# A written-out engine program reordered: about a hundred tasks of block-sparse attention and a squared-ReLU MLP at other places, twelve on other engines

## Chip, cores and metric

The kernel runs on one core of one Trainium2 chip. The metric is the device time of one launch in microseconds (us), lower is better. The core has five engines with a queue each: TensorE (PE, matmuls; PEld is its weight load), VectorE (DVE), ScalarE (ACT), GpSimd (POOL) and SyncE (SP), which here only issues DMAs. POOL issues DMAs too.

## What is computed

Attention of 4 batches, 8 heads, 768 tokens and head size 64, with a block mask (blocks of 32 tokens; a block sees its neighbours, the first and last block, and three sampled blocks), then an MLP with a squared ReLU, 512 to 2048 to 512:

```python
scores = scale * np.matmul(q, k.transpose(0, 1, 3, 2))
mask = np.abs(blk_i - blk_j) <= window
mask = mask | (blk_i == 0) | (blk_j == 0) | (blk_i == n_blocks - 1) | (blk_j == n_blocks - 1)
for qb in range(n_blocks):
    for kb in sampled_blocks[qb]:
        mask[qb * block:(qb + 1) * block, kb * block:(kb + 1) * block] = True
scores = np.where(mask, scores, -1000000000.0)
# softmax over the keys
x = matmul(attn, v), heads side by side: (3072, 512)
h = x @ w_in; r = np.maximum(h, 0.0); g = r * r
return g @ w_out
```

## The kernel before

**Units and batches.** A unit is a pair of heads of one batch: units 0 to 3 are batch 0, 4 to 7 batch 1, 8 to 11 batch 2, 12 to 15 batch 3. Batches 0 and 1 compute all 768 by 768 scores and mask the exponentials. Batches 2 and 3 are sparse: six visits of 128 queries each, for which the keys (`k_gather`, copies on POOL or DVE) and the values (`v_gather`, `v_window`, DMAs from a copy of v in DRAM written by `v_store`) are gathered.

**Getting q, k and v in.** `load` (L150, L152) brings a unit's q, k or v as float32 to SBUF (pools qs, ks, vs), `cast_qk` (L124, L122) makes it bfloat16 in one of four buffers qc, taken in turn, and from unit 4 on `transp_dma` (L313) transposes it by DMA into the resident tile QKT, which frees the qc buffer. Units 0 to 3 are transposed on TensorE (`transp`, L306) and copied out (`evac`). `cast_v` fills VB.

**Attention.** `scores` or `s_scores` (TensorE into one of four PSUM tiles X of two banks), `exps` or `s_exps` on ACT (L358, L624), `masks` or `s_masks` on DVE (L365, L631), then `values` or `s_values` (L204, L396, L654), and `normalize` or `s_normalize` on DVE; the result goes to xT, in batches 1 to 3 through a transposing DMA (L438, L667).

**MLP.** For each of 12 tiles of 256 tokens: 16 tasks `hidden` (four matmul pairs each, xT times w_in), four `relu` (L708 on ACT or L710 on DVE), `square` (L719 ACT, L721 POOL or DVE), 8 tasks `output` (g times w_out), `out_copy` and `store`. The weights come by `w_load` on POOL: pieces 0 and 1 of w_in (L329), 2 to 5 of w_out (L332). The MLP of one batch runs between the attention tasks of the next.

**The order is written out by hand.** The body builds 1224 tasks with their dependencies and buffers, and a string PROGRAM says in which order they are issued. Each word is a letter for the engine (P TensorE, V VectorE, A ScalarE, G GpSimd, S SyncE), the task's number, and for tasks that take a PSUM tile its index after a slash. Every engine runs its own words in that order. Buffers of a pool other than X are handed out in the order of the words, so the order also decides whose release a task waits for:

```python
if b.pool == "X":
    b.at = int(spot)
else:
    b.at = len(taken[b.pool]) % bufs[b.pool]
```

**Tasks named below.** 605 to 636 prepare batch 3: for units 12, 13, 14 and 15 the loads of q, k and v are 605 to 607, 613 to 615, 621 to 623 and 629 to 631; the casts of k and q are 608 and 610, 616 and 618, 624 and 626, 632 and 634; their transposes 609 and 611, 617 and 619, 625 and 627, 633 and 635; the casts of v 612, 620, 628 and 636. 637 and 638 are batch 3's `v_store`. 587 and 565 are `v_window` of batch 2's visits 5 and 4, and 691 of batch 3's visit 2. 642 is the `k_gather` for batch 3's first visit. 571 and 577 are `s_scores` of units 9 and 11 in visit 4, 595, 598, 601 and 579 `s_masks` of batch 2. 986 is a `relu` and 1022 a `hidden` of batch 2's MLP, 980 an `out_copy`. 711 and 712 are the two `v_gather` of batch 3's visit 3, 690 one of visit 2; 700 and 719 are `s_scores` of batch 3. 38 and 39 cast and transpose the later tokens of unit 0's q; 54 casts unit 2's k; 89 copies out a part of the mask; 77 is `w_load(3)`; 793 and 794 are two half `square` tasks.

Of the kernel before, what the change touches and what calls it, by code (L numbers as in the profile page):

```python
# [25 lines left out]
def kernel(  # L26
# [940 lines left out]
    for T in TILES:  # L967
# [48 lines left out]
        P223/3 P203/2 A238 V245 P805 S275 V272 A224 P229/1 P204 P806 S276 A230 V225 S273 G266 P286/3 A823 P807 V231 P808 A287 V205
        P232/1 A829 V270 P206 P289/3 P233 S271 V239 P809 A290 V208 V234 P296/2 V288 S253 A810 P246/3 V291 P235 S437 P247 A297 V236
        P299/0 V248 P830/1 P831 A300 V280 P302/2 V278 P832 A303 S279 P249 P283/0 P833 V250 V298 P852/3 A284 V434 V834 P314/2 S277
        P853 A315 P846/0 S281 V304 P847 A835 P311/1 V285 P854 P855 V258 A312 P848 V301 S269 P849 A856 S21 G282 P292/2 P864/1 V316
        S454 A850 P293 S436 V313 P305/3 P865 V295 A857 G851 P308/0 P306 A309 P866 V307 P353/2 P867 A354 P326/3 G439 V868 P858/0 P859  # L1020
        A327 P320/2 P860 V274 A321 P323/1 V310 S438 P836/3 S444 G441 A324 P861 S460 P347/2 P837 V496 A862 V355 V322 P317/1 A348
        P350/0 S445 V328 P318 V325 G443 P838 S811 V319 A351 V349 P329/2 A869 P334/1 P330 V352 P839 V331 A335 V23 P356/0 S333 A863
        P340/2 P840 A341 P841 G447 P362/1 P357 G459 P842 A363 S452 G449 P337/2 S442 P843 A338 P870/1 A844 S446 V345 P359/2 S448 P871
        A360 V342 V358 P374/3 S462 P872 V339 A375 S440 V336 P365/0 P377/2 V361 P873 A366 V364 P343/3 A378 S450 V367 P371/0 P344 P874
        A372 V346 S845 V376 P368/2 P398/3 V373 P369 A399 P875 S461 V379 S453 V370 P380/0 V470 P401/3 P381 A402 P385/2 V382 P876 V400
        S384 P391/0 P16/3 P877 V451 A392 V403 P404/3 V878 P886/0 A405 P887 A386 V406 G463 P388/1 P425/3 P24/2 P888 A389 G467 V27 V25
        P889 A426 P880/1 P881 S613 G465 A890 S631 P428/3 P882 S469 G455 P883 A429 P407/0 S464 V427 V26 A884 P408 P422/3 V396 A891
        V409 P926/1 P927 V457 A423 P928 V390 S468 P929 A885 V424 P892/2 S456 P893 A930 V387 P413/0 P894 V393 A414 P895 P898/3 V896
        A931 P899 S614 P394/1 P416/0 V430 S466 P395 A417 P900 V397 P932/2 P901 A897 S458 G471 P933 V902 V539 P410/1 P934 A411 G473
        S615 P935 P904/0 S605 V415 A936 P431/3 V502 A903 P905 S472 P432 P476/1 P481/2 P906 A477 V418 A482 P914/1 V412 V433 S621 P915  # L1030
        V498 V541 G499 G937 P419/2 V478 P916 V483 P486/3 P917 A487 P907 A918 P491/3 P420 A492 P479/1 P908 A480 P489/3 P474/1 V421
        P909 A490 V493 S435 A475 P484/2 V488 P910 V545 A485 P911 A919 G503 P920/3 V912 G542 S501 P494/1 G616 P921 G500 V519 P507/2
        P7/0 P922 A508 V495 P513/0 G626 P923 S879 A514 P948/2 V582 S913 G636 P949 A924 S544 P510/1 V515 P504/0 P950 V509 A511 P951
        G620 A505 P954/3 V952 P955 S623 G546 A925 P938/1 S606 S622 V512 P556/0 P939 G523 A557 S497 V506 P553/2 P940 A554 P956 P547/0
        P957 V524 A548 P941 G543 S617 V958 P516/2 V549 S627 P525/0 V558 V584 P942 A526 V517 P550/3 A959 P943 G588 A953 P944 S518
        P528/0 A551 P966/2 P967 A529 V552 P945 V555 S522 G520 P960/3 A946 P968 G618 P531/0 P961 A532 P969 G608 S629 P962 V970 P534/1
        P963 G624 S630 A535 P559/0 V665 A971 V530 S625 G521 P994/2 V589 V562 P995 A964 G566 P988/1 P989 P996 S619 P990 P590/3 G965
        S607 P997 A591 P991 G586 A998 P972/3 G563 P973 A999 V560 P1000/2 V610 P1001 S561 P974 V533 V536 P1002 S609 V992 G628 P593/0
# [3 lines left out]
        P643/0 V667 P1007 V603 A644 P1008 S604 V570 V576 S641 V671 P655/3 P1031 A656 G640 P1034/0 A1032 P1035 V579 P1009 P1036 P1037  # L1042
        P648/3 P1010 A1038 P580/1 A649 G668 A1033 P645/0 P658/3 V688 V581 P1011 A659 V672 P1012 S583 A646 P650/1 P1016/3 A651 P660/0
        P1017 A661 P653/1 P1013 V647 A654 V662 V657 V652 P1018 V692 A1014 P1019 P663/0 V751 A1020 S1015 G693 A1039 P676/1 V664 V710
        P679/2 P1050/3 A677 S670 P1051 A680 G669 P1056/0 P1052 A1021 V681 P1057 P682/1 P1053 S666 A683 P1062/2 V1054 P1063 P1058
        P673/1 S712 P1064 A674 P1059 P1040/3 A1055 V1060 P1065 P1068/1 V684 A1061 P1069 V675 P694/0 P1041 V678 A1066 V714 G715 P1070
        A695 G689 P685/2 A1067 P1071 S981 V753 V686 P703/0 P1042 A1072 S687 P700/2 A704 P1043 V1073 A701 G690 P722/1 P697/0 S756
        P1044 A723 V702 V735 A698 P1045 P716/2 P1046 A717 S713 P725/1 V696 P1047 P1074/0 S691 A1048 P1090/2 A726 P1091 P1084/3 P1085
        S1049 P719/1 P1092 A720 G757 S711 P1075 P1086 V758 P1096/1 V705 P1093 V718 P1097 A1094 V721 P1087 V699 P1098 P1076 A1095
        G736 P1099 A1088 P1102/2 V1100 P1077 P1103 V727 A1101 P706/3 S754 P743/1 V731 P1078 V707 G732 A744 P1104 V724 A1089 P728/3  # L1050
        P1105 V729 P768/1 P1079 A1106 S730 P740/3 G755 A769 P1080 A741 P762/2 S709 P1081 A763 P765/1 P1108/3 V764 A766 S733 V770
        P759/2 P1109 V1082 A760 P746/1 A1107 P1110 V761 V745 A747 P1132/2 V767 P1118/0 V742 S734 P1119 V748 P1133 P1111 P1120 P737/1
        P1134 A738 P1135 P1121 V739 A1136 P1112 V1122 P1139/1 A1137 G1138 P771/2 G1124 P749/0 V772 P1113 G1123 V750 S773 P1140
# [38 lines left out]
```

## Time and profile before

| | us |
|---|---|
| median of three runs | 255.13 |
| the three runs | 257.79, 255.13, 254.16 |
| the profiled execution | 257.6 |
| its span, first to last instruction | 255.9 |
| TensorE busy / idle in the span | 243.9 / 12.0 |
| ACT, DVE, POOL busy | 187.0, 166.3, 106.1 |
| mean granted TensorE clock | 0.992 |

In rows of the waits, "A <- B: total, times, longest" says that A stood idle until B released it; "issue" is time in which nothing that the profile shows was waited for. A row of a timeline has the start, the time, the engine, the line, the operation, out<-in and a count, and in brackets the idle time before it with its releaser. A row of stretches has the stretch, its length, the busy time of TensorE, weight load, DVE, ACT and POOL with their counts, then the granted clock, the share of the DMA engines and GB/s. SPq and POOLq are the parts of an engine that issue DMAs. The 1.7 us between the execution and its span lie before the first and behind the last instruction.

### The profile page before, as it was taken

To read this page: it belongs to the slowest core of one execution; us is meant where nothing else is said; L and a number is where in the kernel's file an instruction comes from. 1 tells how busy PE (TensorE), PEld (TensorE's weight loads), DVE (VectorE), ACT (ScalarE), POOL (GpSimd) and SP (SyncE) were. 2 spreads that over 40 slices of the span, in tenths; PEclk is the share of its full clock that TensorE was granted. 3 is DMA by queue.
4 is the path that set the end of the run, shared out by engine and by line. 5 is a ranking of instruction groups with operands and counts; after the bars stand their busy time and mean duration, and the time that the engine had idled before them with its cause. 6 is when DMAs were issued, how large, how long until landed. Compare 5 with 4: busy or idle time off the path is not lost.

```text
span 255.9 us, 12281 instructions
## 1 busy us (share of the span) xinstructions
PE 243.9 (95%) x5265; PEld 182.1 (71%) x5265; DVE 166.3 (65%) x394; ACT 187.0 (73%) x220; POOL 106.1 (41%) x231
## 2 busy tenths in 40 slices
PE   7988999899999999998999996999999999999994
PEld 4667889679865667776867774867965775776683
DVE  7667997689799989896654964357464555441300
ACT  3898999899998789965867663669887569415241
POOL 3165533010534032579426983347475445140020
PEclk9999999999999999999999999799999999999999
DMA  6999999999899999999999999952548924243022
GB/s 192 356 279 182 200 235 219 254 225 210 238 304 196 258 180 261 160 263 166 287 236 164 178 204 176 259 150 57 158 101 178 219 63 105 66 123 87 3 85 86
DMA packets 64950, 47.10 MB, mean 184 GB/s; under 512 B 32367, under 2 KB 59376, under 8 KB 64896
## 3 DMA queue, kind: packets, MB, share of 16 engines
q1 hardware_dynamic: 58736, 38.02, 67.2%
q0 software_dynamic: 5472, 7.85, 17.1%
q8 instruction: 41, 0.67, 1.1%
q10 hardware_dynamic: 688, 0.46, 0.6%
q14 instruction: 13, 0.11, 0.1%
HBM read 35.51 MB, written 7.91 MB: 170 GB/s over the span
## 4 chain that ended last, share of the span: by engine, by line
PE 73%; DMA 11%; DVE 5%; issue 3%; ACT 2%; POOL 1%; DVEq 1%; SPq 1%; POOLq 0%; ACTq 0%
PE X L204 68%; PE X L654 4%; DMA w_out_sb<-in_moe_w_out_dram 4%; DMA qs<-in_q_dram 3%; DMA KG<-in_k_dram 2%; DMA QKT<-qc 2%; ACT pT L358 1%; DVE r L710 1%; DVE pT L365 1%; DVE qc L124 1%; PE X L396 1%; DVEq L558 1%; POOL g L721 1%; SPq L170 1%; ACT r L708 1%
## 5 line engine op out<-in xcount | busy, mean ns | idle before, releaser
L204 PE MATMUL X<-xT,w_in_sb 64*128 64x256 bf16 x1536 | 99.9, 272 | 1.5 <-DVE r L710 1.2
L204 PE MATMUL X<-w_out_sb,g 64*128 64x512 bf16 (+3 forms) x960 | 95.4, 334 | 1.9 <-issue 1.0
L204 PEld LDWEIGHTS <-w_in_sb 64*128 64x128 bf16 x1536 | 75.4, 95 | 14.8 <-issue 1.9
L358 ACT ACTIVATE pT<-X 128x1024 bf16<-128x1024 f32 x72 | 70.7, 1036 | 7.1 <-PE X L204 5.6
L204 PEld LDWEIGHTS <-g 64*128 64x128 bf16 x960 | 39.4, 94 | 27.9 <-issue 2.4
L624 ACT ACTIVATE pT<-X 128x768 bf16<-128x768 f32 (+1 forms) x56 | 41.3, 767 | 24.5 <-PE X L204 23.9
L719 ACT ACTIVATE g<-r 128x1024 bf16<-128x1024 f32 (+1 forms) x45 | 41.7, 941 | 7.8 <-DVE r L710 7.7
L708 ACT ACTIVATE r<-X 128x1024 f32<-128x1024 f32 x28 | 29.8, 1076 | 14.8 <-PE X L204 14.7
L365 DVE TENSOR_TENSOR pT<-pT,VG 128x1024 bf16<-128x1024 bf16 x60 | 39.6, 696 | 1.5 <-ACT pT L358 1.4
L710 DVE TENSOR_SCALAR r<-X 128x1024 f32<-128x1024 f32 x20 | 24.5, 1223 | 22.8 <-PE X L204 20.7
L581 POOL DMA_DIRECT2D VG<-rows x54 | 27.2, 507 | 22.2 <-issue 8.8
L631 DVE TENSOR_TENSOR pT<-pT,MKS 128x768 bf16<-128x768 bf16 (+1 forms) x48 | 28.2, 624 | 12.3 <-ACT pT L624 11.1
L204 PE MATMUL X<-QKT 64*128 64x256 bf16 (+1 forms) x384 | 32.3, 254 | 2.0 <-issue 0.9
L721 POOL TENSOR_TENSOR g<-r 128x512 bf16<-128x512 f32 (+1 forms) x14 | 16.9, 1220 | 31.2 <-ACT r L708 14.3
L204 PEld LDWEIGHTS <-QKT 64*128 64x128 bf16 x384 | 17.0, 97 | 6.7 <-issue 2.8
L124 POOL CAST VB<-vs 128x768 bf16<-128x768 f32 x10 | 8.4, 842 | 25.5 <-DMA vs<-in_v_dram 25.4
L204 PEld LDWEIGHTS <-pT 64*128 64x128 bf16 x768 | 15.3, 94 | 3.5 <-DVE pT L365 0.2
L204 PE MATMUL X<-VB,pT 64*128 64x65 bf16 x768 | 17.0, 190 | 0.1
L204 PEld LDWEIGHTS <-KG 64*128 64x128 bf16 x528 | 13.5, 95 | 5.0
L204 PE MATMUL X<-QKT,KG 64*128 64x64 bf16 x528 | 15.1, 190 | 0.0
L578 POOL DMA_INDIRECT VG<-rows,idx x9 | 9.0, 1004 | 13.5 <-DMA QKT<-qc 7.7
L124 POOL CAST qc<-ks 128x384 bf16<-128x384 f32 (+1 forms) x15 | 8.0, 566 | 14.6 <-DMA ks<-in_k_dram 12.4
(106 smaller groups left out, 216.1 us busy)
## 6 DMA issues: line engine op xcount, KB each, us to landing
vs<-in_v_dram SPq DMA_DIRECT2D x14, 384.0 KB, 5.0
ks<-in_k_dram SPq DMA_DIRECT2D x13, 384.0 KB, 6.4
qs<-in_q_dram SPq DMA_DIRECT2D x12, 384.0 KB, 4.7
out_dram<-ys SPq DMA_DIRECT2D x9, 512.0 KB, 5.8
VG<-rows SPq DMA_DIRECT2D x20, 132.0 KB, 4.0
w_in_sb<-in_moe_w_in_dram POOLq DMA_DIRECT2D x2, 1024.0 KB, 9.3
w_out_sb<-in_moe_w_out_dram POOLq DMA_DIRECT2D x4, 512.0 KB, 9.4
VG<-rows POOLq DMA_DIRECT2D x54, 33.0 KB, 3.2
```

The lines of the kernel that those rows point to most:

```text
L124: (V if e == "DVE" else G).tensor_copy(out=out, in_=in_)
L204: last = nc.tensor.matmul(out(r ^ crossed), lhsT(r ^ crossed, rows), rhs(r ^ crossed, rows), skip_group_check=True, **kw)
L358: A.activation(out=pT[:, :, 0:n], in_=stile.pop(a)[:, :, 0:n], func=AF.Exp, scale=scale)
L365: V.tensor_tensor(out=pT, in0=pT, in1=m[:, None].broadcast_to([P, 2, len(cs), w]), op=AOP.mult)
L581: (G if e == "POOL" else sy).dma_start(out=to[j * HB:(j + 1) * HB], in_=pairs[bass.ds(r * HB, HB)])
L624: A.activation(out=pT[:, :, 0:n], in_=stile.pop((u, v, gs))[:, :, 0:n], func=AF.Exp, scale=scale)
L631: V.tensor_tensor(out=pT, in0=pT, in1=m[:, None].broadcast_to([P, 2, n]), op=AOP.mult)
L654: nc.tensor.matmul(po[i * D:(i + 1) * D, h, a * VW:(a + 1) * VW], pts[g][:, h, c * D:(c + 1) * D], val, start=a == 0 and c == 0, stop=c == ...
L708: A.activation(out=to, in_=src, func=AF.Relu)
L710: V.tensor_scalar(out=to, in0=src, scalar1=0.0, scalar2=None, op0=AOP.max)
L719: A.activation(out=g, in_=r, func=AF.Square)
L721: (G if e == "POOL" else V).tensor_mul(out=g, in0=r, in1=r)
```

## The change

Only PROGRAM changes: all 1224 tasks remain, with the same dependencies. The indices of the PSUM tiles are permuted throughout. Twelve tasks go to another engine: 54 (`cast_qk`), 912 (`out_copy`) and 992 (`relu`) from DVE to ACT; 89 (`mask_evac`) and 1072 (`relu`) from ACT to DVE; 256, 278 and 457 (`cast_qk`) from DVE to POOL; 455 (`cast_qk`) and 628 (`cast_v`) from POOL to DVE; 443 (`cast_v`) from POOL to ACT; 712 (`v_gather`) from SyncE to POOL. About a hundred keep their engine and stand elsewhere in its queue, most of them a few places away.

On SyncE, from the load of unit 15's q on, the order

    629 630 625 619 607 561 609 611 540 633 587 635 565 637 638 947 604

becomes

    629 607 609 619 630 561 611 625 540 587 633 565 637 638 947 635 604

and further on 712 leaves, and 691 moves from behind 713 to ahead of 687. On VectorE `632 634 708 595 986 598 601 980 573` becomes `628 632 595 986 708 598 601 980 579 634 573`. On TensorE `977 599 978 979 571 1022 1028 1029 1023 577` (with 574 ahead of 977) becomes `977 599 574 978 571 577 979 1028 1029 1022`. On POOL `787 793 794 77` becomes `787 794 77 793`, `690 757` becomes `690 712 757`, and 38 goes from behind 73 to ahead of 49.

The lines of the diff that hold these places:

```diff
-    P4/3 P9/1 P125/3 V41 A116 P2/1 P106/2 V3 G52 A126 G74 G63 P5/0 V107 P123/1 P65/0 A124 P108 P121/3 V66 V110 G49 P82/0 A122
-    P84/2 P131/1 V83 G60 V85 P135/0 A132 G73 P86/3 P117/2 V87 A136 G38 P88/1 G75 P10/3 P133/3 V118 A89 P61/0 A134 G78 P119 V62
-    P12/1 P90/1 V120 P168/0 G76 P15/2 P39/3 A91 P174/2 V40 A169 P127/1 G70 A175 P137/3 V128 P144/0 V138 P129 P147/2 A145 V130
+    A114 G64 P9/2 P125/0 P2/2 A116 V3 G52 P106/3 A126 P5/2 P123/1 V107 G63 P65/2 A124 P108 P121/0 V110 G74 V66 P82/3 A122 P84/1
+    V83 G38 P131/2 V85 P135/3 A132 P86/0 P117/1 V87 A136 G49 P10/2 V118 P88/0 P133/2 G60 V89 P12/3 A134 G73 P61/3 P119 P90/0 V62
+    A91 P39/2 G75 V120 P168/3 V40 P174/1 A169 P127/0 G78 P137/2 G76 A175 V128 P144/3 G70 V138 P129 P147/1 A145 V130 V176 P15/0
...
-    V160 A216 P98/2 P190/0 V163 A99 P212/3 V792 A780 P164/2 A213 S81 V191 P795/1 G793 A779 V165 P796 P209/3 G794 P192 P166 S259
-    S260 P797 A210 V167 V193 P798 P824/2 V217 V214 V383 A799 G77 P825 P197/0 P194/3 P826 G801 A198 P827 P818/1 A195 V828 G254
+    S251 S252 P190/3 V163 A99 P212/2 V792 A780 P164/1 A213 V191 P795/0 G794 A779 V165 P796 P209/2 P192 P166 P797 G77 A210 V167
+    V193 V214 P798 V217 S81 P824/1 G793 V383 A799 P825 P194/3 P826 A195 G801 P827 S259 S260 P197/2 S267 P818/0 A800 V828 G254
...
-    P963 G624 S630 A535 P559/0 V665 A971 V530 S625 G521 P994/2 V589 V562 P995 A964 G566 P988/1 P989 P996 S619 P990 P590/3 G965
+    P966/2 P967 A529 V552 P945 V555 G520 P960/1 A946 S522 P968 G618 P531/3 P961 A532 P969 G624 P962 S629 V970 P559/0 G608 S607
...
-    P1003 G585 A594 S611 V527 A1004 G612 G564 A993 P537/1 V567 A1005 P982/0 V639 P983 P596/2 P975 V538 A597 P984 V592 S540 P976
-    V632 P568/2 P985 S633 A569 V634 P574/1 P977 V708 V595 P599/2 P978 V986 A600 S587 P979 A575 V598 S635 A987 V601 P571/2 V980
-    A572 S565 P1022/0 V573 P1028/1 P1029 S637 P1023 S638 P577/3 P1030 A578 G642 P1024 S947 P1025 P1006/2 A1026 P602/3 A1027
+    P1003 P537/2 S625 A1004 P982/0 V639 V538 A993 P983 P596/3 V592 P975 A1005 S540 G585 V628 V632 P984 A597 P976 G612 S587 V595
+    P568/2 P985 A569 P977 S633 V986 V708 P599/3 P574/2 P978 A600 V598 S565 G564 A575 V601 P571/0 P577/3 P979 A572 A578 V980
+    P1028/2 A987 P1029 S637 V579 V634 S638 S947 V573 P1022/0 S635 P1030 P1023 P1031 G642 P1024 A1032 P1025 P1006/3 A1026 P602/1
...
-    P673/1 S712 P1064 A674 P1059 P1040/3 A1055 V1060 P1065 P1068/1 V684 A1061 P1069 V675 P694/0 P1041 V678 A1066 V714 G715 P1070
+    P1045 V1073 P719/1 G712 P716/0 S756 P1046 V724 A717 V702 P725/3 A720 P1047 V735 S713 P1074/0 A1048 P1090/1 A726 V696 P1091
...
-    P1044 A723 V702 V735 A698 P1045 P716/2 P1046 A717 S713 P725/1 V696 P1047 P1074/0 S691 A1048 P1090/2 A726 P1091 P1084/3 P1085
+    P1059 A674 P1064 V1060 P1040/2 A1055 P1065 V684 A1061 S981 P1068/0 V714 G715 G689 S691 P1069 A1066 P694/1 V675 P1041 V678
```

More of the change, by code (lines that the diff above doesn't have):

```diff
@@ L1016 @@
[L1016 to L1023, printed above, removed]
@@ new lines @@
+        P139 P71/0 A148 V140 P171/3 V170 P781/2 P782 V72 A172 V146 P92/1 P187/0 P783 V93 A188 P784 V173 P50/3 P181/1 A785 P177/0
+        V189 V51 A182 P141/2 G786 V178 P774/3 P775 A142 V149 P184/1 P179 P776 G79 G22 V180 A185 P94/2 P777 V143 P155/0 A95 V778 G787
+        P150/1 A156 P158/2 V151 P161/3 A159 P788/0 V183 P152 P789 S80 V186 A154 P215/2 A162 P790 V157 P14/1 P791 V160 A216 P98/1
+        S251 S252 P190/3 V163 A99 P212/2 V792 A780 P164/1 A213 V191 P795/0 G794 A779 V165 P796 P209/2 P192 P166 P797 G77 A210 V167
@@ new lines @@
+        V193 V214 P798 V217 S81 P824/1 G793 V383 A799 P825 P194/3 P826 A195 G801 P827 S259 S260 P197/2 S267 P818/0 A800 V828 G254
+        P819 A198 G256 P226/3 S255 P820 A227 P200/1 V196 P812/2 V211 P813 S257 A201 P243/3 V199 P821 P814 A244 V264 P218/1 P815 S265
+        A822 P219 P802/3 A816 V220 S268 V202 P240/0 P221 P803 A241 V228 P96/2 P804 A222 V97 A817 S261 P237/0 V262 P223/1 P203/2 A238
+        V242 S263 P805 V245 A224 P229/0 P204 S275 P806 A230 V225 V272 P286/1 A823 P807 V231 S276 V205 S273 P808 A287 G266 P232/0
@@ new lines @@
+        A829 P289/1 V270 P233 V239 P206 P809 A290 S271 V208 V234 P296/2 A810 P246/1 V288 S253 P235 P247 G278 V236 S437 A297 P299/3
+        P830/0 V291 S279 P831 A300 V248 P302/2 P832 V280 A303 S277 P249 P283/3 V250 P833 V298 S281 P852/1 A284 V434 V834 P314/2 P853
+        A315 P846/3 V304 P847 A835 P311/0 V285 P854 V258 P855 A312 P848 V301 S269 P849 S21 A856 V316 P292/2 V313 P864/0 A850 P293
+        G282 P305/1 V295 A857 P865 S454 G851 P308/3 S436 P306 A309 P866 V307 P353/2 P867 A354 P326/1 G439 V868 P858/3 P859 A327
@@ new lines @@
+        P320/2 P860 V274 A321 P323/0 V310 S438 P836/1 S444 V355 A324 P861 S460 V322 P347/2 S445 P837 V496 A862 G441 P317/0 A348
+        P350/3 V328 P318 V325 S811 P838 A351 V319 V349 P329/2 A869 P334/0 V352 P330 P839 V331 A335 V23 P356/3 S333 A863 P340/2 P840
+        G447 P841 A443 G449 P362/0 A341 P357 P842 G459 S452 A363 S442 P337/2 P843 A338 P870/0 S446 A844 S448 P359/2 P871 V345 A360
+        V342 P374/1 S845 P872 V358 A375 V336 S462 P365/2 P377/3 S440 V339 P873 A366 V361 P343/1 A378 V364 P371/2 P344 V367 P874 A372
@@ new lines @@
+        S450 V346 P368/3 V376 P398/2 P369 S461 V373 A399 P875 S453 V379 P380/1 V370 V470 P401/2 P381 A402 P876 V382 V400 P391/3 S384
+        P385/1 P877 A392 P404/2 V878 P16/3 A405 P886/3 P887 V403 A386 P425/0 P24/2 P888 P388/1 P889 G463 A426 V451 V406 A389 P880/0
+        S613 P881 V26 G467 A890 S631 P428/1 P882 G465 S469 P883 A429 P407/3 V455 G457 S464 A884 V27 P408 P422/1 V396 V427 V25 A891
+        P926/0 P927 A423 P928 S468 V409 A885 P929 V390 P892/2 S456 A930 V424 P893 P413/1 V387 P894 A414 P895 V393 P898/3 A931 V896
@@ new lines @@
+        P899 S614 P394/0 P416/1 V430 S466 P395 P900 A417 V397 P932/2 G471 P901 S458 A897 P933 V902 V539 G473 P410/0 P934 A411 P935
+        P904/1 V415 S605 A936 V502 S472 P431/3 A903 P905 P432 V418 P476/0 P481/2 P906 A477 V412 V433 S621 V498 V541 A482 G499 P914/0
+        S615 P915 V483 P419/3 P916 P486/2 P917 A487 P907 A918 P491/2 P420 A492 P479/0 P908 A480 G616 G937 V421 G503 P489/2 S435 V488
+        P474/3 P909 A490 V493 G500 V478 V545 A475 P484/0 P910 A485 S501 P911 A919 P920/2 G620 A912 P494/3 G542 S879 G626 P921 V519
@@ new lines @@
+        S1049 S711 G757 P1084/2 P1085 V758 P1092 V705 P1075 V718 V721 P1086 P1096/3 V699 P1093 P1097 A1094 P1087 G736 P1098 S754
+        P1076 A1095 P1099 A1088 P1102/1 V1100 P1077 P1103 A1101 V727 P706/2 P728/3 V731 V707 G732 P1104 V729 P765/2 P1078 A766 S730
+        P743/3 P1105 A744 P768/2 P1079 A1089 S709 P1080 A1106 G755 P762/3 P1081 A769 S733 P1108/1 A763 P759/2 V764 P740/3 P1109 A760
+        V770 V1082 A741 P1110 A1107 S734 P1132/2 V761 P1118/3 V745 P1119 V767 P746/0 P1133 V742 A747 P1111 V748 P1120 P737/0 P1134
@@ new lines @@
+        A738 P1135 P1121 V739 A1136 P1112 V1122 P1139/0 A1137 G1138 P771/2 G1124 P749/3 V772 G1123 P1113 V750 S773 P1140 P1125/2
+        S752 P1126 P1141 P1142 S1083 P1127 A1143 P1128 P1114 V1129 G1144 P1115 A1131 P1156/3 A1116 P1157 P1146/0 A1145 S1117 P1158
+        A1130 P1163/2 P1159 P1164 V1160 P1147 P1148 A1162 A1161 P1177/1 P1165 P1178 P1170/3 P1171 P1179 P1180 P1149 V1181 P1172
+        P1173 P1166 A1174 P1150 V1167 P1151 A1169 G1168 P1152 A1183 P1153 A1176 G1175 A1182 P1184/1 A1154 P1185 P1186 S1155 P1187
@@ L1060 @@
+        P1194/3 P1195 P1188 P1196 P1197 P1189 P1190 P1191 P1198 A1192 P1199 P1200 P1201 S1193 P1214/2 P1215 A1202 P1216 P1217 S1203
+        P1218 P1219 P1204/0 P1205 P1206 P1207 P1220 P1221 P1208 P1209 A1222 P1210 P1211 P8/1 S1223 P6/3 P13/2 P17/1 V1212 S1213
     """
```

49 lines of the change are left out of this document (12 added, 37 removed).

## The prediction

> **What bounds the kernel now.** I read the page's first part, then the stretches of 8 us, then the waits, then the timeline where TensorE stands still.
>
> ```profile
> PE 243.9 (95%) x5265; PEld 182.1 (71%) x5265; DVE 166.3 (65%) x394; ACT 187.0 (73%) x220; POOL 106.1 (41%) x231
> ```
> ```profile
> 40.00:48.00 8.00, 7.26 (x156) 5.82 (x152) 6.33 (x11) 8.00 (x11) 1.09 (x2) 1.00 1.17 207
> ...
> 152.00:160.00 8.00, 5.78 (x104) 3.49 (x100) 4.30 (x8) 3.95 (x6) 3.13 (x7) 0.97 1.23 171
> 160.00:168.00 8.00, 8.00 (x150) 6.10 (x151) 3.70 (x8) 5.32 (x6) 2.19 (x9) 0.82 0.99 249
> ```
> ```profile
> PE X L204 <- issue: 1.9, 2, 1.0
> ```
>
> TensorE is busy for 243.9 of the span of 255.9 us (front table), and no matmul is added or removed. A reordering can therefore win only from the 12 us of idle and from matmuls that run slowly. The worst stretch is 152 to 168: TensorE busy for 5.78 of 8 us, then a granted clock of 0.82. Here is what happens in it.
>
> ```profile
> 152.55 1.00 DVE L124 CAST qc<-ks 128x384 bf16<-128x384 f32 x2
> 157.25 1.01 DVE L124 CAST qc<-qs 128x384 bf16<-128x384 f32 x2 [3.70 <-issue]
> 158.18 0.55 DVE L631 TENSOR_TENSOR pT<-pT,MKS 128x768 bf16<-128x768 bf16 x1
> 158.65 1.22 DVE L710 TENSOR_SCALAR r<-X 128x1024 f32<-128x1024 f32 x1
> ```
> ```profile
> 155.46 0.81 PE L204 MATMUL X<-w_out_sb,g 64*128 64x512 bf16 x6
> 157.30 1.26 PE L204 MATMUL X<-w_out_sb,g 64*128 64x512 bf16 x10 [1.03 <-issue]
> ```
> ```profile
> 159.92 3.38 PE L204 MATMUL X<-xT,w_in_sb 64*128 64x256 bf16 x32 [1.19 <-DVE r L710]
> ...
> 168.46 1.47 PE L204 MATMUL X<-xT,w_in_sb 64*128 64x256 bf16 x24
> ```
> ```profile
> 159.90:163.00 3.10, 3.08 (x30) 2.56 (x31) 2.50 (x4) 1.75 (x2) 2.19 (x9) 0.51 1.28 243
> ```
>
> VectorE's queue runs in order. The cast of unit 15's q (task 634, at 157.25) stands still for 3.70 us. Its load was issued long before, so I read the wait as one for its qc buffer, which the transpose of unit 12's k (609) has to empty; that is an inference, since the row names no releaser. Behind the cast stands the relu 986 (158.65), and TensorE waits 1.19 us for the bank that it frees. Then 32 matmuls take 3.38 us under a clock of 0.51; at the rate of the 24 in 1.47 us they would take 1.96. The event costs 1.19 + 1.42 = 2.61 us. The 1.03 us before 157.30 falls inside one group of matmuls and has no releaser.
>
> **Part by part.** *The cast 634 and the last batch on SyncE.* Six DVE tasks that stood behind 634 now stand ahead of it (595, 986, 598, 601, 980, 579). From 152.55 on DVE runs a cast of v (628, moved from POOL), the cast 632, one mask multiply (0.55, as at 158.18) and the relu 986.
>
> ```profile
> L124 DVE CAST VB<-vs 128x768 bf16<-128x768 f32 x4 | 2.2, 551 | 0.0
> ```
> The relu ends at 152.55 + 0.55 + 1.00 + 0.55 + 1.22 = 155.87 instead of 158.65 + 1.22 = 159.87. The first TensorE task that needs its bank is now the scores task 571, which follows the group of eight begun at 155.46; that group would end near 156.3. So the wait goes, with 0.4 us to spare: **-2.6**. What must hold is that 632 does not wait itself. Its load (630) has moved behind one load and two transposes:
>
> ```profile
> 139.63 0.37 SPq L152 DMA_DIRECT2D ks<-in_k_dram  x1
> 140.52 4.70 SPq L313 DMA_TRANSPOSE QKT<-qc  x2
> ```
> ```profile
> ks<-in_k_dram SPq DMA_DIRECT2D x13, 384.0 KB, 6.4
> ```
> It is issued at about 145.2 (140.52 + 4.70) and lands, with the median 6.4, at 151.6. It is needed at 152.55 + 0.55 = 153.1: 1.5 us to spare. The load of v (607) takes the place that 630 had, so the five transfers are the old five in another order. If 630 is later than that, 595 and 986 queue behind 632 on DVE, and TensorE behind 986.
>
> Transposes 625, 633 and 635 are later on SyncE too: 633 stands behind the two DMAs of v_window 587, 635 behind both v stores and an output store. Their readers:
>
> ```profile
> QKT<-qc SPq DMA_TRANSPOSE x24, 6.5
> ```
> ```profile
> 160.66 0.40 POOL L593 COPY KG<-QKT 128x256 int32<-128x256 int32 x1 [3.26 <-DMA QKT<-qc]
> ```
> ```profile
> 168.38 0.25 PE L204 MATMUL X<-QKT,KG 64*128 64x64 bf16 x6
> ...
> 173.62 0.34 PE L204 MATMUL X<-QKT 64*128 64x64 bf16 x12
> ```
> POOL's key gather (642, at 160.66) waits for 633 already, and TensorE reads its result at 168.38, 7.7 us after POOL begins it. 633 issued 2 us later costs nothing there. 635 is read at 173.62; it waits for 634, now near 160, and lands, with the median 6.5, by 168: nothing. The v stores lose 635 ahead of them and can only be earlier.
>
> The clock is where a rule changes the sum. By the Trainium skill, "TensorE: Matmul & The Clock Gate", section "What's actually happening", the array drops to half rate only after an idle window of about 3.4 us and returns after a busy one. The 0.51 over 3.10 us agrees with the half and the length, but the idle stretches are 1.03 and 1.19 us, shorter than its window. By that rule the half clock is not the 1.19's doing, and this term would be -1.2.
>
> *w_load(3) one square earlier on POOL.*
>
> ```profile
> 35.85 2.04 POOL L721 TENSOR_TENSOR g<-r 128x512 bf16<-128x512 f32 x2 [4.55 <-DVE rs L408]
> 37.84 0.81 POOL L332 DMA_DIRECT2D w_out_sb<-in_moe_w_out_dram  x1
> ```
> ```profile
> 47.03 1.04 PE L204 MATMUL X<-w_out_sb,g 64*128 64x512 bf16 x8 [0.73 <-DMA w_out_sb<-in_moe_w_out_dram]
> ```
> Two squares take 2.04, so the issue comes 1.0 us earlier, and TensorE's wait of 0.73 goes if the landing follows. Bounds: 0 (the transfers share busy DMA engines, 1.17 in the row for 40 to 48) and -0.73. I take **-0.7**, since the issue moves by more than the wait. The square that goes behind the DMA is needed by the output part after the one at 47.03, about 9 us later: nothing.
>
> *The head.*
>
> ```profile
> 17.23 1.36 POOL L124 CAST qc<-qs 128x512 bf16<-128x512 f32 x2 [1.75 <-DMA qs<-in_q_dram]
> ...
> 19.31 0.61 POOL L124 CAST qc<-qs 128x512 bf16<-128x512 f32 x1
> ```
> ```profile
> 18.65 0.29 PE L306 MATMUL X<-identb,qc 64*128 64x64 bf16 x8 [0.53 <-POOL qc L124]
> ```
> The cast at 19.31 (unit 0, whose part was loaded first) moves into POOL's idle 1.75 us, and its transpose moves ahead of a task that waits anyway: it takes TensorE 0.29 in a gap. Against it, cast 54 moves to ACT, which runs exps back to back there. ACT shows no such size: 0.51 for half the columns and 1.04 for a larger activation bound it.
>
> ```profile
> L122 ACT CAST qc<-ks 128x384 bf16<-128x384 f32 x1 | 0.5, 512 | 1.6 <-DMA ks<-in_k_dram 1.6
> ```
> ```profile
> L358 ACT ACTIVATE pT<-X 128x1024 bf16<-128x1024 f32 x72 | 70.7, 1036 | 7.1 <-PE X L204 5.6 <-PE X L425 0.6 <-ACT g L719 0.3
> ```
> I take 0.8, nearer the larger size. A mask evacuation (89) leaves ACT for DVE, and TensorE waits for POOL at 18.65 in any case. Bounds +0.8 and -0.5, taken **-0.3**.
>
> *The other engine moves* (256, 278, 443, 455, 457, 912, 992, 1072). Each puts a task of about 1 us on another of DVE, ACT and POOL.
>
> ```profile
> 72.00:80.00 8.00, 8.00 (x196) 4.89 (x190) 7.17 (x24) 7.05 (x8) 3.35 (x6) 1.00 1.20 262
> 112.00:120.00 8.00, 7.12 (x154) 4.68 (x150) 6.50 (x15) 5.86 (x8) 7.67 (x17) 1.00 1.22 200
> 144.00:152.00 8.00, 7.98 (x165) 5.89 (x163) 5.79 (x15) 5.72 (x7) 7.66 (x11) 1.00 1.07 169
> ```
> ACT takes a cast (443) in the first of these, an output copy (912) in the second and a relu (992) in the third; it has 0.95, 2.1 and 2.3 us free in them. 256, 278 and 457 go to POOL, which is busy 1.09 in the row for 40 to 48. Nothing; without that cover about 1 each.
>
> *v_gather 712 from SyncE to POOL.*
>
> ```profile
> 186.24 4.33 SPq L581 DMA_DIRECT2D VG<-rows  x6
> ```
> ```profile
> 194.15 3.43 POOL L581 DMA_DIRECT2D VG<-rows  x6 [1.95 <-issue]
> 200.39 0.40 POOL L593 COPY KG<-QKT 128x256 int32<-128x256 int32 x1 [2.81 <-PE X L204]
> ...
> 208.44 3.43 POOL L581 DMA_DIRECT2D VG<-rows  x6 [3.30 <-PE X L204]
> 213.74 3.43 POOL L581 DMA_DIRECT2D VG<-rows  x6 [1.87 <-issue]
> ```
> ```profile
> VG<-rows POOLq DMA_DIRECT2D x54, 33.0 KB, 3.2
> ```
> ```profile
> 223.15 1.83 PE L654 MATMUL X<-VG,pT 128*64 128x65 bf16 x96
> ```
> POOL's last gather ends at 217.17 and lands at 220.4; TensorE reads it at 223.15: 2.8 us to spare. 712 adds 3.43 + 1.95 = 5.4. POOL gets back what it waited for TensorE behind 690: down to the ordinary gap of 1.87, that is 2.81 - 1.87 plus 3.30 - 1.87 = 2.4, since the scores task 719 is earlier too. 5.4 - 2.4 - 2.8 = **+0.2**. Bounds: 0, and +2.6 if nothing comes back. SyncE is relieved of 4.33, so v_window 691 and gather 711 come earlier.
>
> The Trainium skill speaks against this move: "SBUF — State Buffer", section "SBUF: two separate sides", has DMAs issued from GpSimd starve while VectorE holds the port pair that they share. The trace shows gathers of 3.43 us on POOL with DVE active; by that rule they could stretch, and the term would grow.
>
> *About 40 small swaps on TensorE's queue.* A task that comes earlier can meet a bank not yet freed, by an ACT task of 1.04 at most. Clearest is scores 700, one exp behind: 0.2. Together **+0.3** (0 to 1).
>
> **Sum.** The profiled execution took 257.6: 257.6 - 2.6 - 0.7 - 0.3 + 0.2 + 0.3 = **254.5**. The median of the runs shown, 255.1, lies 2.5 below that execution, about the size of the event at 157 to 163. If plain runs lack the event, 255.1 - 0.7 - 0.3 + 0.5 = 254.6: the same.
>
> **Rivals.**
> *A. 632 waits in 634's place (slower).* If load 630 lands after 153.5, 8.3 us after its issue, the relu is late again and TensorE pays the 2.61: 254.5 + 2.6 = **257.1**. For it: the DMA share of 1.23 and the 3.70 us that a transpose could take too long. Against it: the same five transfers are only permuted.
> *B. POOL becomes the bound in the last batch.* No wait comes back, TensorE stands 2.6 instead of 0.2 at 223: **256.9**. For it: gaps of 1.9 at every gather. Against it: 2.8 us of room.
> *C. The waits of 1.9 us without releaser go as well.* Both occur under heavy DMA; a shift of the transfers could end them: **252.6**. Against it: the DMA load is the same.
> *D. Nothing is gained.* The event was that one execution's, and the two small gains are covered: 255.1 + 0.5 = **255.6**.
>
> **How the numbers follow.** Forecast 0.40, A 0.14, B 0.14, C 0.12, D 0.14, two of A, B and the clock together 0.06. Two per cent, about what a measurement of this kernel can tell from no change, is 250.0 and 260.2. Faster than that needs C and more: 0.06. Slower needs A and B at once: 0.07. The range reaches from below C to above A: 251.8 to 257.5.
>
> **What would show it.** DVE should have no wait of 3 us near 157; the relu rows there should lie before 156.3, with a clock of 1.00 from 160 to 168. The wait for w_out_sb should be gone from TensorE's list. POOL should show one gather more between 194 and 204, and TensorE no wait for VG at about 221. I am wrong if VectorE waits at the k cast instead, or if TensorE's new order meets full banks in the head.

## The result, and the profile after

The changed kernel takes **254.03 us** (median of 20 runs, 252.01 to 257.37) against 257.87 for the kernel before (20 runs, 254.16 to 262.42). The ratio is 0.992, 95% interval 0.9892 to 0.9948; in a second comparison it was 0.9858 (0.9791 to 0.9924). So it is 0.5 to 2% faster. Medians here are over all runs; the ratios leave out each kernel's runs of more than 1.5% above its fastest, so a ratio differs from the quotient of two medians, here 0.985. The first three runs of before had a median of 255.13, which the longer series corrects to 257.87, next to the profiled execution (257.6).

The page's first part, then the same stretches of 8 us as before (stretch, length, busy time of TensorE, weight load, DVE, ACT, POOL, granted clock, DMA share, GB/s):

```profile
span 251.2 us, 12279 instructions
## 1 busy us (share of the span) xinstructions
PE 240.7 (96%) x5265; PEld 181.8 (72%) x5265; DVE 159.7 (64%) x392; ACT 188.4 (75%) x222; POOL 109.8 (44%) x237
```
```profile
40.00:48.00 8.00, 7.89 (x161) 5.67 (x156) 6.49 (x10) 7.99 (x11) 2.62 (x3) 1.00 1.15 224
...
152.00:160.00 8.00, 8.00 (x164) 6.13 (x162) 5.81 (x10) 5.56 (x8) 4.53 (x8) 1.00 1.24 153
160.00:168.00 8.00, 8.00 (x192) 5.17 (x190) 2.85 (x13) 4.95 (x8) 4.25 (x14) 1.00 1.14 264
```

From 152 to 168 TensorE is now busy throughout at a clock of 1.00; before it had 5.78 of 8 us and then 0.82. The timeline of DVE shows why:

```profile
151.00 1.00 DVE L124 CAST qc<-ks 128x384 bf16<-128x384 f32 x2
151.93 0.56 DVE L631 TENSOR_TENSOR pT<-pT,MKS 128x768 bf16<-128x768 bf16 x1
153.08 1.22 DVE L710 TENSOR_SCALAR r<-X 128x1024 f32<-128x1024 f32 x1 [0.60 <-PE X L204]
...
157.98 1.00 DVE L124 CAST qc<-qs 128x384 bf16<-128x384 f32 x2
```

The cast 632 (151.00) did not wait, the relu 986 ended at 154.30, and the cast 634 (157.98) ran behind it without a wait. The 0.60 ahead of the relu is now DVE waiting for TensorE. New places of idle TensorE:

```profile
8.29 0.35 PE L306 MATMUL X<-identb,qc 64*128 64x64 bf16 x12 [1.27 <-DVE qc L124]
...
59.28 0.29 PE L204 MATMUL X<-QKT 64*128 64x256 bf16 x2 [0.55 <-issue]
```
```profile
185.51 0.25 PE L654 MATMUL X<-VG,pT 128*64 128x65 bf16 x3
186.27 0.89 PE L654 MATMUL X<-VG,pT 128*64 128x65 bf16 x45 [0.51 <-DMA VG<-rows]
```

The first, in the head, does not come from the head's new order: two of the profiles below with the old head have 0.97 and 1.00 there.

### The profile page after: what moved, and what is told of

Same layout as the page of the kernel before. It is cut to its first block, busy times and chain, and to the rows that moved or that the text cites. A ratio compares the mean times of both kernels' runs of the same rounds, so it can differ in the third digit from the quotient of the medians.

```text
span 251.2 us, 12279 instructions
## 1 busy us (share of the span) xinstructions
PE 240.7 (96%) x5265; PEld 181.8 (72%) x5265; DVE 159.7 (64%) x392; ACT 188.4 (75%) x222; POOL 109.8 (44%) x237
## 4 chain that ended last, share of the span: by engine, by line
PE 70%; DMA 10%; issue 8%; DVE 3%; ACT 3%; POOL 2%; SPq 1%; POOLq 1%; DVEq 0%; ACTq 0%
PE X L204 65%; PE X L654 3%; DMA QKT<-qc 3%; DMA qs<-in_q_dram 3%; DMA KG<-in_q_dram 2%; ACT pT L358 2%; DMA VG<-rows 2%; PE X L396 2%; DVE pT L365 1%; SPq L170 1%; DVE r L710 1%; POOL g L721 1%; POOLq L558 1%; POOL KG L599 1%; ACT r L708 1%
## 5 line engine op out<-in xcount | busy, mean ns | idle before, releaser
L204 PE MATMUL X<-xT,w_in_sb 64*128 64x256 bf16 x1536 | 98.9, 269 | 0.5 <-ACT r L708 0.3
L204 PEld LDWEIGHTS <-g 64*128 64x128 bf16 x960 | 41.1, 94 | 24.9 <-PE X L204 0.2
L365 DVE TENSOR_TENSOR pT<-pT,VG 128x1024 bf16<-128x1024 bf16 x60 | 40.8, 716 | 1.3 <-ACT pT L358 1.3
L710 DVE TENSOR_SCALAR r<-X 128x1024 f32<-128x1024 f32 x20 | 24.5, 1224 | 26.2 <-PE X L204 21.2
L708 ACT ACTIVATE r<-X 128x1024 f32<-128x1024 f32 x28 | 29.5, 1072 | 14.9 <-PE X L204 14.9
L581 POOL DMA_DIRECT2D VG<-rows x60 | 29.4, 496 | 18.7 <-issue 10.4
L631 DVE TENSOR_TENSOR pT<-pT,MKS 128x768 bf16<-128x768 bf16 (+1 forms) x48 | 24.7, 550 | 13.8 <-ACT pT L624 12.7
L204 PE MATMUL X<-QKT 64*128 64x256 bf16 (+1 forms) x384 | 31.7, 250 | 0.9 <-issue 0.5
L721 POOL TENSOR_TENSOR g<-r 128x512 bf16<-128x512 f32 (+1 forms) x14 | 17.5, 1255 | 29.3 <-DVE r L710 16.8
L124 POOL CAST qc<-ks 128x384 bf16<-128x384 f32 (+1 forms) x14 | 7.3, 551 | 20.8 <-DMA ks<-in_k_dram 14.0
L124 POOL CAST VB<-vs 128x768 bf16<-128x768 f32 x8 | 6.6, 829 | 19.2 <-DMA vs<-in_v_dram 19.2
L599 POOL COPY KG<-QKT 128x64 int32 x66 | 14.6, 269 | 0.0
```

The source lines that it names most:

```text
L124: (V if e == "DVE" else G).tensor_copy(out=out, in_=in_)
L204: last = nc.tensor.matmul(out(r ^ crossed), lhsT(r ^ crossed, rows), rhs(r ^ crossed, rows), skip_group_check=True, **kw)
L365: V.tensor_tensor(out=pT, in0=pT, in1=m[:, None].broadcast_to([P, 2, len(cs), w]), op=AOP.mult)
L581: (G if e == "POOL" else sy).dma_start(out=to[j * HB:(j + 1) * HB], in_=pairs[bass.ds(r * HB, HB)])
L599: eng.tensor_copy(out=rows[:, :, :, r_ * w:(r_ + 1) * w], in_=src[:, :, :, bass.ds(at[r_] * w, w)])
L631: V.tensor_tensor(out=pT, in0=pT, in1=m[:, None].broadcast_to([P, 2, n]), op=AOP.mult)
```

## The experiments

Twelve kernels ran in three sets, each beside the kernel before on its chip (its medians: 257.89, 258.25, 257.79).

| kernel | median | ratio to before | interval | wait of cast 634 in its profile |
|---|---|---|---|---|
| before | 257.87 | | | 3.70 |
| changed, first series | 254.03 | 0.9920 | 0.9892 to 0.9948 | none |
| changed, again | 254.74 | 0.9858 | 0.9791 to 0.9924 | none |
| last batch's part alone | 254.76 | 0.9838 | 0.9771 to 0.9905 | none |
| changed without that part | 256.57 | 0.9937 | 0.9897 to 0.9977 | 0.71 |
| before, cast 634 later | 256.27 | 0.9881 | 0.9832 to 0.9930 | none |
| before, transpose 609 earlier | 257.05 | 0.9979 | 0.9923 to 1.0034 | none |
| last batch's part, 634 early again | 259.81 | 1.0038 | 0.9994 to 1.0082 | 2.45 |
| before, cast 264 later | 256.50 | 0.9918 | 0.9867 to 0.9970 | none |
| before, 264 and 634 later | 257.13 | 0.9980 | 0.9932 to 1.0029 | none |
| part around 77 alone | 256.67 | 0.9927 | 0.9880 to 0.9974 | 3.71 |
| before, 77 earlier | 258.66 | 0.9961 | 0.9906 to 1.0015 | none |
| head's part alone | 257.87 | 0.9979 | 0.9930 to 1.0028 | 1.88 |
| changed, end undone | 256.00 | 0.9908 | 0.9853 to 0.9962 | none |

**The last batch's part alone, and the change without it.** The first takes the orders from task 629 to batch 3's first visit into the old program, on all engines; the second puts the old ones into the changed program.

> The kernel before with the last batch's part of the change alone (the engine orders from the load of unit 15's q to the scores of batch 3's first visit; everything ahead of it and behind it as before). The theory of the prediction: the cast 634 no longer stands ahead of the relu 986, no wait of 3 us at 634, the relu ends before 156.5, TensorE has neither the wait of 1.19 nor a clock of 0.51 there: 1.2 (wait alone) to 2.6 us less than before, ratio 0.990 to 0.995. Rival D (the event belonged to the one profiled execution of before): within 0.4 us of before, ratio 0.998 to 1.002, and what the whole change gains comes from elsewhere. Rival C (the two waits without releaser follow the transfers): the wait of 1.03 near 157 is gone here too, the one of 0.88 near 116 stays, since the transfers ahead of it are those of before.

> The changed kernel with the last batch's part put back to the old orders. The theory of the prediction: 634 waits over 3 us again and TensorE over 1 us behind the relu 986; 1.2 to 2.6 us slower than the changed kernel, which leaves 0 to 0.8 us of gain against before (ratio 0.997 to 1.000). Rival D: as fast as the changed kernel, ratio to before about 0.992.

The part alone gives as much as the whole change, and more than the 0.990 to 0.995 that I had expected. Its relu and TensorE's tasks stand as in the changed kernel; this is its stretch table:

```profile
152.00:160.00 8.00, 8.00 (x160) 6.09 (x158) 6.20 (x11) 5.71 (x8) 4.63 (x8) 1.00 1.27 160
```

The change without the part keeps 0.6%, nearer to rival D's 0.992 than to the 0.997 to 1.000 that I had expected. And its profile lacks the great wait, although VectorE has the old order:

```profile
153.02 1.00 DVE L124 CAST qc<-ks 128x384 bf16<-128x384 f32 x2
154.73 1.01 DVE L124 CAST qc<-qs 128x384 bf16<-128x384 f32 x2 [0.71 <-issue]
```

So the wait is not a fixed cost. With the old place of 634 on VectorE and the old order on SyncE it is 3.70, 3.71, 1.88, 0.71, 0 and 0 in six profiles. TensorE waits behind the relu in the first two of them, 1.19 in the kernel before and 1.44 in the part around 77:

```profile
160.56 1.92 PE L204 MATMUL X<-xT,w_in_sb 64*128 64x256 bf16 x32 [1.44 <-DVE r L710]
```

**One task on VectorE, one on SyncE.**

```diff
 V  632 [-634-] 708 595 986 598 601 980 [+634+] 573        (cast later; S635 behind S947)
 S  629 [+609+] 630 625 619 607 561 [-609-] 611            (transpose earlier)
```

> The kernel before with one task moved on VectorE: the cast 634 goes behind 595, 986, 598, 601 and 980, and its transpose 635 behind the store 947 on SyncE, as it must; SyncE's order is otherwise the old one. The theory of the prediction (the place on VectorE is what counts): the relu 986 ends near 155.4, the wait of 1.19 is gone, and this alone gives what the last batch's part gives, within 0.5 us. The rival (the order on SyncE counts): less than half of it. The wait of 1.03 without releaser has nothing to do with VectorE and stays.

> The kernel before with one task moved on SyncE: the transpose 609 goes ahead of the load 630 and of 625, 619, 607 and 561, some 7 us earlier. VectorE keeps its order. If the 3.70 us at the cast 634 were a wait for the qc buffer that 609 empties, as the prediction inferred, the wait is under 0.3 us here, the relu 986 ends near 156.3 and TensorE's wait of 1.19 is gone or under 0.3. If 634 waited for something else (its load, SyncE), it still stands for 3 us. In time the first gives as much as moving the cast, the second nothing.

With the cast later the ratio is 0.9881, about three quarters of the part's gain (by the medians half of it, 1.5 us short of the part, where I had expected 0.5 at most), and 152 to 168 is full (PE 8.00 and 8.00). The wait of 1.03 without releaser, which I had expected to stay, is not in this profile either. With the transpose earlier 634 waits for nothing:

```profile
152.71 1.00 DVE L124 CAST qc<-ks 128x384 bf16<-128x384 f32 x2
153.63 1.00 DVE L124 CAST qc<-qs 128x384 bf16<-128x384 f32 x2
```

That fits **a wait for the buffer that 609 empties**, but alone does not show it, since two profiles with the old order have no wait either. By the order of the words, which hands out the four buffers in turn, 634 does get the buffer of 608, which 609 empties; and the wait is back in the next kernel, in which a later transpose empties it. In time the earlier transpose brings 0.2%, not told from nothing, against the expectation. Moving the transpose takes away this wait; 634 still stands ahead of the relu.

**The part, with 634 early again.**

```diff
 V  628 632 [+634+] 595 986 708 598 601 980 579 [-634-] 573
```

> The last batch's part alone, as in the first set, but with the cast 634 directly behind the cast 632 on VectorE again. SyncE's new order issues the transpose 609, which empties 634's buffer, some 7 us earlier, so 634 should not wait over 0.5 us. Theory that SyncE's order alone suffices: the relu 986 is one cast (1.00 us) later at most, TensorE waits under 0.5 us for it, the stretch 152 to 168 stays busy for 15.5 of 16 us or more and the time is that of the part alone (ratio 0.981 to 0.991). Rival (the place on VectorE is what counts): TensorE waits 0.5 to 1.2 for the relu 986 and at least half of the gain is lost (ratio over 0.992).

Without the cast's new place the rest of the part, SyncE's new order with it, is worth nothing: 1.0038 against 0.9838, with intervals apart, for one task. (The two ran in different sets on two chips, each beside the kernel before.) I had expected no wait at 634, since 609 is early. It waited 2.45:

```profile
155.13 1.01 DVE L124 CAST qc<-qs 128x384 bf16<-128x384 f32 x2 [2.45 <-issue]
156.06 0.55 DVE L631 TENSOR_TENSOR pT<-pT,MKS 128x768 bf16<-128x768 bf16 x1
156.52 1.22 DVE L710 TENSOR_SCALAR r<-X 128x1024 f32<-128x1024 f32 x1
```
```profile
157.79 0.53 PE L204 MATMUL X<-QKT,KG 64*128 64x64 bf16 x24 [1.82 <-DVE r L710]
```
```profile
146.37 3.32 SPq L313 DMA_TRANSPOSE QKT<-qc  x2
```

The new order also puts cast 624 ahead of 608, so 634 takes 624's buffer, and 625 empties it: the second of the two transposes issued from 146.37, 8 us later than 609. The change makes the buffer come free no earlier; it takes the waiting cast out of the way. This profile shows how the cast holds up TensorE, 1.82 us, but not what a usual run of this kernel pays: the profiled execution took 255.05, the fastest of its twelve runs, whose median is 259.81.

**Another cast of the same kind.** In the profile of the kernel with 634 later, TensorE lost more elsewhere. DVE, then TensorE:

```profile
41.24 0.68 DVE L365 TENSOR_TENSOR pT<-pT,VG 128x1024 bf16<-128x1024 bf16 x1
44.83 0.56 DVE L124 CAST qc<-qs 128x768 bf16<-128x768 f32 x1 [2.92 <-DMA qs<-in_q_dram]
45.31 0.68 DVE L365 TENSOR_TENSOR pT<-pT,VG 128x1024 bf16<-128x1024 bf16 x1
```
```profile
46.05 0.84 PE L204 MATMUL X<-VB,pT 64*128 64x65 bf16 x24 [2.34 <-DVE pT L365]
```

Cast 264 waits for its load, a mask queues behind it, TensorE behind the mask. The change puts 264 behind two masks; this run puts it behind three and the cast 256.

```diff
 V  196 [-264-] 211 256 228 199 [+264+] 220
```

> The kernel before with one task moved on VectorE: the cast 264 (unit 5's q) goes from ahead of the masks 211, 228 and 199 to behind them, its transpose 265 to behind the load 267 as before; nothing else. In the kernel with the cast 634 moved, 264 waited 2.92 us for its load, TensorE 2.34 us for the mask 211 behind it, and the clock was 0.5 for the next 3.41 us. Theory of the late transfers (each cast on VectorE that is fed by a DMA and stands ahead of masks is a risk, not a fixed cost): faster than before by 0.3 to 1.5 us in the median, ratio 0.994 to 0.999, and no wait for mask 211 in its profile. Rival (that wait was a chance of one execution, as good as never in before): within 0.3 us.

> The kernel before with the two casts 264 and 634 behind the masks (and the relu 986) that they stood ahead of, and nothing else of the change. Theory of the late transfers: the gains of the two add up, 1.5 to 3 us less than before, at least two thirds of what the changed kernel beside it gains. Rival (the gain is spread over the hundred moves, the last batch's on SyncE above all): about 1 us, under half of it.

264 later gives 0.3 to 1.3%. Both casts together should have given two thirds of the whole and gave 0.2%, within noise of nothing. In that profile TensorE waited elsewhere: 0.91 for a transposed x, and 1.34 inside one task, without a releaser.

```profile
160.31 1.92 PE L204 MATMUL X<-xT,w_in_sb 64*128 64x256 bf16 x32 [0.91 <-DMA xT<-XS]
...
166.52 0.48 PE L654 MATMUL X<-VG,pT 128*64 128x65 bf16 x19 [1.34 <-issue]
```

SyncE's order around them was the old one. Why two moves that each gain bring nothing together stays open; that other waits took the place is seen in this one execution (258.5, above the kernel's median) and not shown as the cause.

**The load 77 and the part around it.**

```diff
 G  787 [-793-] 794 77 [+793+]
```
(The part around it also moves, among others, 256 to POOL, 264 behind two masks and some loads on SyncE.)

> The kernel before with the part of the change around the load of w_out's piece 3 (task 77 a square earlier, the cast 256 on POOL, the cast 264 two masks later, some loads on SyncE in another order). The prediction's term: TensorE's wait of 0.73 for that piece is gone, 0.7 us less; with the late-transfer theory 0.3 to 1 us more on top, since 264 stands behind mask 211 here too: ratio 0.993 to 0.997. Rival (covered by the transfers themselves, the landing does not come earlier): no change, ratio 0.998 to 1.001, with a wait for w_out_sb of 0.5 us or more.

> The kernel before with two words exchanged on POOL: the load of w_out's piece 3 (77) ahead of the square 793. The prediction's term: the wait for w_out_sb at 47 goes, 0.7 us less. What the profiles so far show: without that wait TensorE stands 0.4 to 0.9 at 57 to 59, which has no releaser and ends 1.4 to 1.5 us after a block of its instructions has landed; the stretch 40 to 64 as a whole is no better. So the theory now is: the wait at 47 is under 0.3, a new one stands at 57 to 59, the time within 0.5 us of before (ratio 0.996 to 1.002). Rival (the prediction): 0.7 us less, ratio 0.996 to 0.998 with no new wait.

Both profiles have lost the wait for w_out_sb at 47. The exchange alone: no measurable gain; its profile has 264's wait (2.07) and TensorE's 1.49 behind it, and no new wait at 57, so my expectation of one was wrong for this kernel. The whole part gains 0.3 to 1.2%, with 264 later in it, and does have the new wait:

```profile
59.21 0.29 PE L204 MATMUL X<-QKT 64*128 64x256 bf16 x2 [0.92 <-issue]
```

Of five profiles with the whole part four have it (0.55 and 0.79 in the changed kernel, 0.92 here, 1.20 with the end undone); the fifth has 0.65 at 64 instead. Without the part none has more than 0.38 there.

**Head and end.**

> The kernel before with the head's part of the change alone (cast 38 and transpose 39 earlier, cast 54 on ACT, the mask copy 89 on VectorE, some swaps ahead of 24 us). The prediction's term: 0.3 us less (0.5 less to 0.8 more). TensorE's idle and slow time ahead of 24 us is 5.6 to 6.6 in all profiles so far, with no order between old and new, so the rival is nothing at all: ratio 0.997 to 1.002. What decides the head's profile is then where the first half clock falls, which is no property of the order.

> The changed kernel with its end put back (the gather 712 on SyncE, v_window 691 behind 713, the swaps from 180 us on). The prediction's term: the end costs 0.2 and some swaps, so this kernel is 0 to 0.5 us faster than the changed one. Both profiles of the changed kernel show TensorE waiting at 186 for VG (0.51 and 1.11), which the prediction did not have; if that is the end's doing, the wait is under 0.3 here and the time 0.5 to 1 us lower than the changed kernel's, ratio to before 0.982 to 0.990. Rival (the wait comes with being early, whatever the end's order): the same wait, the same time.

The head's part: 0.9979, which holds both the 0.3 us and nothing. Undoing the end shows no gain. TensorE's wait for VG near 186 goes with neither order of the end. The profile with the end undone has none, but neither has that of the change without the last batch's part, which keeps the new end; and it is 0.92 in the profile of the old program with only 77 moved:

```profile
189.61 0.89 PE L654 MATMUL X<-VG,pT 128*64 128x65 bf16 x45 [0.92 <-DMA VG<-rows]
```

"The changed kernel, again" was run for this comparison.

> The changed kernel itself, beside the others of this set on the same chip. Both theories: 0.984 to 0.992 of before, as in its own comparison and in that of the last batch's part. Its profile should again have no wait of over 2 us on TensorE and no clock of 0.5 ahead of the end. The theory that single late transfers make the difference would also allow one such event at a place where a cast fed by a load stands ahead of masks on VectorE.

Its profile has no wait over 2 us and no half clock ahead of the end.

## Why the prediction was right, step by step

The forecast was 254.5; 254.03 was measured. It had 3.1 us go from the profiled execution; the median lost 3.84. That the sum comes so near is in part luck. Its start, 257.6, lay 2.5 above the median then known and happened to lie next to the long series' median (257.87); and T1 was too small, while the other terms, -0.5 together, did not show in the whole: the last batch's part alone gives as much as the whole change.

*T1, the cast 634 (-2.6).* Every link is seen in the traces: the buffer, VectorE's order, the relu, TensorE. The point that I had named as its condition held too: 632 did not wait for the load 630 (rival A). (Eight matmuls of the group at 155.46 take 1.03, so it would have ended near 156.5 and not 156.3; nothing hangs on that.) The size was off: the part alone is worth 1.6% (1.0 to 2.3), that is 4.2 us (2.4 to 5.9) of 257.9, and moving 634 back costs 2% (259.81 against 254.76). Rival D saw one half of this: the event does not occur each time. But it is not one execution's either: three of the six waits above are 1.88 or more.

What makes the price so large stays open. In the six profiles TensorE paid 2.61 and 1.44 us, which is 0.7 us on the mean. The granted clock of every single run is on record too. It is below 0.995 in 46 of 92 runs of the kernel before in the three sets, in 7 of 26 of the changed kernel, in 1 of 6 of the part alone, and in 9 of 12 with 634 early again; but in only 2 of 12 of the changed kernel without the part, where the cast has its old place as well. So the half clock does not simply go with the cast's place. One stretch of 3.41 us at half clock is worth 1.7 us, and among the runs at 0.995 or more the changed kernel is ahead all the same: medians of 253.6 and 254.6 against 256.8 to 257.2. Most of the gain is therefore not the half clock, and the profiles, one or two of each kernel, do not show where the rest lies.

Where the 3.70 us came from was not in the prediction. This is the DMA view of before from 154.2 to 157.4, 40 slices of 0.08 us; a packet is booked in the slice in which it starts:

```profile
DMA  9999192999090000000010000002009090299999
GB/s 125 144 336 48 3 35 51 262 282 914 0 158 0 0 0 0 0 0 0 0 10 6 10 10 6 10 10 56 0 0 686 0 845 0 7 210 166 278 266 291
...
q8 instruction: 1, 0.02, 2.8%
```

From 155.2 to 155.8 no packet starts, and from there to 156.4 only small ones, at 6 to 10 GB/s. By the packet records one block (16 KB) on the queue that brings instructions (q8) ran from 154.41 to 155.83, and the small ones, the last 20 packets of the transposes, ran one behind the other from 155.81 to 156.40. DVE's cast began at 157.25, TensorE went on at 157.30. In the part around 77, where 634 waited 3.71 and TensorE 0.81 without a releaser, the records show the same (block to 156.40, tail to 156.94). So in these two profiles **the wait "without releaser" and the one at the cast go together**: as I read it, TensorE's next instructions came late, and a transpose's tail stood behind them. The kernel with the head's part (1.88) has such a tail too, from 153.66 on behind a block that ends at 153.66, but no wait of TensorE with it. In two profiles with waits of 0.71 and 0 the transposes had ended at 154.25 and 154.28, when the block had just begun (154.23) or not yet (154.94). That the tail waited *because* it shared a DMA engine with the block is inferred from this order; packets of a gather on POOL's queue were under way until 156.6 as well, and no run separates the two.

*Rival C* therefore half came true. In the changed kernel's first profile both such waits are gone (1.9 us), and that execution ran in 252.8, near C's 252.6; but 0.55 of the kind stands at 59.28, and 0.79 in the second profile (255.01). They move from profile to profile: the part alone and the kernel with 634 later have none over 0.2, the kernel with the end undone has 1.20.

*T2, the load 77 (-0.7).* Its own wait goes, as said, but with the whole part 0.55 to 1.20 come back at 58 to 59, and the wait was 0.4 to 0.7 only in some profiles with the old place and absent in others. The failed step is "-0.7, since the issue moves by more than the wait": it priced the wait and not what is late next.

*T3, the head (-0.3)* was too small to be told from nothing. *T4, 712 to POOL (+0.2):* no wait for VG at 221, POOL one gather more (each still 3.43 to 3.44), no price found. Rival B is out.

*The 40 small swaps on TensorE's queue (+0.3)* were not run alone. What the prediction got wrong here is a step that stands in none of its terms: 264 behind two masks on VectorE. Alone, behind three, it is worth 0.3 to 1.3%, a gain, though with 634 it brought nothing. The same question, asked of 634, was not asked of the other casts on VectorE that wait for a DMA.

The parts do not add up: last batch 1.6%, the part around 77 0.7%, the head 0.2%, the whole 0.8 to 1.4%. The engine moves of the middle (278, 443, 455, 457, 912) were not run alone.

## What to carry to other kernels

On an engine that works in order, a cast that waits for a DMA can cost what stands behind it, with the tail of the landing time and not its median. Put it behind the work that the bound engine waits for, even at no gain in the profile at hand, and measure each such move together with the others: here two that each gained brought nothing together. When tasks that take buffers in turn are exchanged, look up anew whose release each waits for. And before pricing a stall from one profile, see whether it stands in a second one.

## What the runs showed of the hardware

**The clock.** In these traces its steps lie on a grid of 3.41 us. With stretches laid on that grid, the first of each pair is the one with the idle time, the second what followed: before, the kernel with 634 later, the one with 77 earlier, and the part around 77.

```profile
156.11:159.53 3.42, 1.59 (x24) 0.89 (x22) 2.28 (x4) 1.06 (x2) 0.48 (x1) 1.00 1.07 204
159.53:162.94 3.41, 3.02 (x30) 2.50 (x31) 2.87 (x5) 1.75 (x2) 2.19 (x9) 0.50 1.26 229
```
```profile
42.58:45.99 3.41, 1.13 (x22) 0.77 (x16) 1.16 (x3) 2.51 (x3) 0.00 (x0) 1.00 1.38 235
45.99:49.41 3.42, 3.36 (x62) 2.37 (x64) 2.53 (x7) 1.02 (x1) 0.00 (x0) 0.50 1.00 255
```
```profile
43.08:46.49 3.41, 1.92 (x70) 1.46 (x68) 2.63 (x5) 2.15 (x4) 0.00 (x0) 1.00 1.21 213
46.49:49.90 3.41, 3.41 (x58) 1.99 (x56) 3.05 (x8) 3.13 (x5) 0.00 (x0) 1.00 1.03 230
```
```profile
158.04:161.45 3.41, 1.98 (x39) 1.55 (x35) 3.41 (x7) 0.91 (x1) 0.14 (x1) 1.00 1.20 204
161.45:164.87 3.42, 3.28 (x64) 2.66 (x58) 1.59 (x2) 2.14 (x4) 2.04 (x9) 1.00 1.16 255
```

Busy for 1.13 or 1.59 of 3.41, TensorE ran the next stretch at half clock; busy for 1.92 or 1.98 it did not. The part around 77 had waits of 0.81 and 1.44, the kernel before 1.03 and 1.19, about the same sum. In the part around 77 they fell into two stretches of the grid; in the kernel before 1.83 us of them fell into one. So whether a wait of 1.2 costs another 1.4 depends on where the grid lies, which changes from run to run. Behind the first 20 us no profile speaks against this; in the head two profiles drop after 1.2 to 1.3 us of idle time and the changed kernel does not after 1.36. The prediction's rule from the Trainium skill ("TensorE: Matmul & The Clock Gate", "What's actually happening") has a free-running window of 3413 ns, which agrees; that the whole window must be idle does not: 1.83 us of idle time was enough, and the term of 1.42 did belong to the event.

**TensorE's instructions.** By the Trainium skill ("Runtime: NRT & Kernel Launch", "Instruction fetch mechanics") crossing a block of 16 KiB is mostly hidden. The trace agrees on the block and shows where it is not hidden: TensorE stood 0.88 and 1.03 in before and 0.55 in the changed kernel, each until 1.4 to 1.5 us after a block had landed.
